# A written list of 1905 numbers takes the place of the planner that ordered a linear-attention and FFN kernel

## The chip, the core and the metric

The kernel runs on one core of one Trainium2 chip. The metric is the device time of one execution in microseconds (us); less is better. A core has five engines that run side by side, each with an instruction queue of its own: PE (TensorE, matrix products), DVE (VectorE), ACT (ScalarE), POOL (GpSimd) and SP (SyncE, which here only issues DMAs). In the source they are called `PE`, `V`, `A`, `G` and `Q`.

## The reference

```python
def _A_ref(x, wqkv, w_phi, wo):
    B, S, D = x.shape; H = 32; Dh = D // H
    q, k, v = (x @ wqkv).reshape(B, S, 3, H, Dh) ...          # 2048 rows of 512, 32 heads of 16
    pq = jnp.einsum("bhsd,hdf->bhsf", q, w_phi)
    pk = jnp.einsum("bhsd,hdf->bhsf", k, w_phi)
    phi_q = jnp.concatenate([_softmax(pq), _softmax(-pq)], axis=-1)
    phi_k = jnp.concatenate([_softmax(pk), _softmax(-pk)], axis=-1)
    kv = jnp.einsum("bhsf,bhsd->bhfd", phi_k, v)
    z  = jnp.einsum("bhsf->bhf", phi_k)
    num = jnp.einsum("bhqf,bhfd->bhqd", phi_q, kv)
    den = jnp.einsum("bhqf,bhf->bhq", phi_q, z)[..., None] + 1e-6
    return (num / den) ... @ wo

def _B_ref(x, w1, b1, w2):                                     # F = 1792
    h = jnp.einsum("bsd,df->bsf", x, w1) + b1
    sp = jnp.log1p(jnp.exp(-jnp.abs(h))) + jnp.where(h > 0, h, 0)
    return jnp.einsum("bsf,fd->bsd", h * jnp.tanh(sp), w2)

x  = A_x                       # (1, 2048, 512)
xn = _layernorm(x)
return x + _A_ref(xn, ...) * silu(_B_ref(xn, ...))
```

All arrays are float32.

## The kernel before

The 2048 rows of `x` are 16 tiles of 128. Each float32 factor of a large product is split into a high and a low part of a shorter format, and each product is three matmuls (low by high, high by low, high by high), mostly 128x512 to a call; 1944 such calls make up nearly all of PE's work. The products for keys and values and both layers of the FFN are done with seven half-sized products in place of eight, so that sums and differences of tiles and of weights (`ts`, `ws`, `wss`, `w1s`, `w2s`) are needed, and each of these is split in its turn: ACT writes the high part (`th`, `w1sh`), and DVE or POOL subtracts it to get the low part (`tl`, `wss`, `w1sl`, `w`).

The stages, in the order in which PE goes through them: first the weights are folded (`wkf`, `wqf`) and the 16 tiles are normalized (`norm`, L517 on) and transposed on PE (`pt`, then `xT`); among and after these come the projections (`k`, `q`, `v`, and `kx`, `ky`, `kz`) and the sums over keys (`kvp`); then FFN layer one (`fx`, `fy`, `fz`), whose transposed inputs go out to DRAM and come back as `fb0h` to `ft3l`; then layer two (`y`, `z`, `x`), mixed with the attention's numerators (`pn`) and output products (`pw`, which read `oh` and `ol`); last `u` and `xx`, the joining of both branches.

In `norm`, DVE finds mean and variance (`st`, `mv`), adds a constant (`rs`), POOL takes the power -1/2 of `rs`, DVE computes `nb` = -mean times `rs` (L528 on, a `scalar_tensor_tensor` of 128x1), and ACT or DVE normalizes the tile; with ACT that is one activation with `nb` as its bias. Only then can PE transpose the tile.

What sets the order: the body doesn't issue anything. Each call on an engine is recorded (`Program.call`, L110); calls inside `one()` (L132) become one operation, and where these calls are on two engines, the operation can run on either: `either` is DVE or POOL, `copy` is ACT or DVE. There are 1905 operations. `ORDER` (L38) names the parts of the work in a row, and so fixes the order in which operations are recorded. PE's operations keep that order. For the four other engines `simulate` (L178) goes through the program with a cost for each operation and picks, whenever an engine is free, the operation whose latest start is earliest; of two engines that can do an operation, the one that gets to it first takes it, and DVE's bid for one that POOL can do counts as 8000 ns later (`PEN`). `issue` (L345) then emits all operations in the order of their simulated starts; their instructions all carry line 352. On the chip each engine goes through its row strictly in order and waits where an input isn't there yet.

Of the kernel before, what the change touches and what calls it, by code (L numbers as in the profile page):

```python
# [54 lines left out]

class Program:


    def __init__(self, nc):
        self.eng = {"PE": nc.tensor, "V": nc.vector, "G": nc.gpsimd, "A": nc.scalar, "Q": nc.sync}  # L60
        self.ops, self.tag, self.cap, self.pe = [], {}, {}, []
        self.group, self.slack, self.part, self.half = None, SLACK, None, 0

    @staticmethod
    def cost(e, m, a, k):
        aps = [v for v in a if isinstance(v, bass.AP)]
        n = aps[0].free_size()
        if e == "PE":
            if m == "transpose":
                return 109  # L70
            n, c = aps[2].free_size(), aps[1].free_size()
            if aps[1].dtype == F32R:
                return max(n / 2.4 + 0.104 * c, c * 0.835 + 2)
            full = 2 * max(n / 1.2 + 2.5, c * 0.835)
            if aps[1].shape[0] == 32:
                return max(full / 16, 27)
            return max(full * aps[0].shape[0] / P, 27)
        if e == "Q":
            return 450
        if e == "A":  # L80
            return (60 if aps[1].space == "PSUM" else 110) + 0.833 * n + 93 * (len(aps) - 2)
        psum = any(v.space == "PSUM" for v in aps[1:])
        nn = max(v.free_size() for v in aps)
        if e == "V":
            if m == "reciprocal":
                return 70 + 6.3 * n
            if m in ("tensor_scalar", "tensor_copy") and not psum:
                return 70 + 0.52 * n
            return 70 + 1.04 * nn
        if k.get("op") == ALU.pow:  # L90
            return 520
        return (140 + 1.73 * n) if bcast(a) else (140 + 2.17 * n)

    @staticmethod
    def records(m, a, k):

        return 2 if m == "transpose" or a[1].dtype == F32R else 4

    def add(self, impl, reads, writes, sets=()):
        o = Op()  # L100
        o.code = sum(self.records(*c) for c in impl["PE"][1]) if "PE" in impl else 0
        o.impl, o.reads, o.writes, o.idx, o.sets, o.slack = impl, reads, writes, len(self.ops), sets, self.slack
        o.pos, o.part, o.half = len(self.pe), self.part, self.half
        self.half = 0
        o.lock = {e for e, (_, calls) in impl.items() if any(locks(e, m, a) for m, a, k in calls)}
        if "PE" in impl:
            self.pe.append(o)
        self.ops.append(o)

    def call(self, e, m, a, k):  # L110
        aps = [v for v in list(a) + list(k.values()) if isinstance(v, bass.AP)]
        w = {box(aps[0])}
        r = {box(v) for v in aps[1:]}
        c = self.cost(e, m, a, k)
        s = [ACT_SET[a[2]]] if e == "A" and a[2] in ACT_SET else []
        if self.group is None:
            self.add({e: (c, [(m, a, k)])}, r, w, s)
        else:
            g = self.group
            g[0].setdefault(e, [0, []])  # L120
            g[0][e][0] += c
            g[0][e][1].append((m, a, k))
            g[1].update(r)
            g[2].update(w)
            g[3].extend(s)

    def halves(self, k):

        self.group[0]["PE"][0] += SWITCH[k]
        self.half = SWITCH[k]  # L130

    @contextmanager  # L132
    def one(self):
# [6 lines left out]
        g, self.group = self.group, None  # L140
        self.add({e: tuple(v) for e, v in g[0].items()}, g[1], g[2], g[3])

    def order(self):
        at = [0]
        for o in self.pe:
            at.append(at[-1] + o.impl["PE"][0])
        self.links()
        return self.simulate(at)

    def links(self):  # L150
        ops = self.ops
        wr, rd = {}, {}
        for o in ops:
            o.succ, dep = [], set()
            for n in o.reads:
                dep.update(i for i, m in wr.get(n[0], ()) if meet(n, m))
            for n in o.writes:
                dep.update(i for i, m in wr.get(n[0], ()) if meet(n, m))
                dep.update(i for i, m in rd.get(n[0], ()) if meet(n, m))
            dep.discard(o.idx)  # L160
            if "PE" in o.impl:
                dep = {d for d in dep if "PE" not in ops[d].impl}
            for d in dep:
                ops[d].succ.append(o)
            o.deps = len(dep)
            for n in o.reads:
                rd.setdefault(n[0], []).append((o.idx, n))
            for n in o.writes:
                wr.setdefault(n[0], []).append((o.idx, n))
        self.uses, self.first = {}, {}  # L170
        for o in ops:
            o.tiles = {n[0] for n in o.reads | o.writes if n[0] in self.tag}
            for n in o.tiles:
                self.uses[n] = self.uses.get(n, 0) + 1
                if n not in self.first:
                    self.first[n] = o
# [917 lines left out]
```

## Time and profile before

| | before |
|---|---|
| median of 3 runs | 507.02 us (506.91 to 510.05) |
| the profiled execution | 507.63 us |
| its span, first to last instruction | 505.6 us |
| PE busy | 488.1 us (97%), 3126 matmuls and transposes |
| DVE busy | 430.8 us (85%), 571 instructions |
| POOL busy | 396.8 us (78%), 264 instructions |
| ACT busy | 280.6 us (56%), 418 instructions |
| DMA | 115.54 MB, mean 229 GB/s |
| mean granted TensorE clock | 0.992 |

The span is what the profile shows of the profiled execution; 2.0 us of its time lie outside it. Busy times are sums of durations. Those of PE are modelled at their ends, and DVE's overlap a little from one instruction to the next, so that a sum can come out above what the engine was really taken for. "Idle before" stands in square brackets in the timeline, with the name of what ended it.

### The profile page before, as it was taken

What the parts mean: (1) busy time and instruction counts of PE and PEld (TensorE: products, weight loads), DVE (VectorE), ACT (ScalarE), POOL (GpSimd) and SP (SyncE); (2) the same over time, 40 slices, a digit from 0 to 9 for tenths busy, and PEclk for the clock granted to TensorE, in tenths of its full rate; (3) what the DMA queues carried; (4) which work ended last, traced back from release to release, by engine and by line L of the source; (5) the groups of instructions that cost most, each with busy time, mean ns of one, the idle gap of its engine ahead of it and who ended that gap; (6) DMA issues with size and microseconds to landing.
All of it is one profiled execution on the core that took longest, in us unless ns stands there. A gap on an engine that the chain in (4) does not pass through costs nothing.

```text
span 505.6 us, 8592 instructions
## 1 busy us (share of the span) xinstructions
PE 488.1 (97%) x3126; PEld 399.4 (79%) x3126; DVE 430.8 (85%) x571; ACT 280.6 (56%) x418; POOL 396.8 (78%) x264
## 2 busy tenths in 40 slices
PE   9986999999999899999999999999999999999993
PEld 9765888888888787888888877888888886788882
DVE  5988899999998869978999898998668568779993
ACT  4864745555354335245423587566796657758420
POOL 2797766989999777657978796977895578799990
PEclk9999899999999999999999999999999999999998
DMA  8775562445683989997899697275964934476375
GB/s 311 244 260 189 198 221 102 160 153 209 219 290 93 324 300 287 288 331 251 278 320 351 202 361 284 83 244 186 312 204 132 376 124 154 148 246 210 105 216 178
DMA packets 64985, 115.54 MB, mean 229 GB/s; under 512 B 6960, under 2 KB 31152, under 8 KB 64944
## 3 DMA queue, kind: packets, MB, share of 16 engines
q1 hardware_dynamic: 64800, 114.98, 66.3%
q8 instruction: 24, 0.39, 0.3%
q14 instruction: 17, 0.14, 0.1%
q10 hardware_dynamic: 144, 0.03, 0.0%
HBM read 72.92 MB, written 42.07 MB: 227 GB/s over the span
## 4 chain that ended last, share of the span: by engine, by line
PE 86%; DVE 7%; ACT 2%; POOL 1%; DMA 1%; issue 0%; ACTq 0%
PE y L352 19%; PE fx L352 14%; PE pw L352 9%; PE fy L352 8%; PE x L352 7%; PE kx L352 7%; PE q L352 7%; PE ky L352 4%; PE fz L352 3%; PE pn L352 2%; PE z L352 2%; PE kz L352 2%; PE kvp L352 2%; DVE nb L352 1%; DMA ft1l<-scrT 1%; PE wake L352 1%
## 5 line engine op out<-in xcount | busy, mean ns | idle before, releaser
L352 PE MATMUL q<-wqh,xT 128*128 128x512 f32 x128 | 43.3, 404 | 0.0
L352 ACT ACTIVATE r<-r,b1t 128x512 f32<-128x512 f32 x56 | 37.9, 714 | 9.1 <-DMA r<-hd 8.8
L352 PEld LDWEIGHTS q<-wqh,xT 128*128 128x128 f32 x128 | 24.8, 194 | 5.2
L352 PE MATMUL q<-wql,xT 128*128 128x512 f32 x64 | 25.6, 400 | 0.0
L352 POOL TENSOR_TENSOR rs<-rs,mhalf 128x1 f32<-128x1 f32 x16 | 10.9, 685 | 12.7 <-DVE rs L352 12.7
L352 ACT ACTIVATE hb<-fx 128x512 f32<-128x512 f32 x14 | 8.3, 597 | 22.4 <-PE fx L352 20.2
L352 DVE TENSOR_REDUCE tz<-ez 128x64 f32<-128x1024 f32 x16 | 19.4, 1211 | 0.4 <-POOL ez L352 0.3
L352 ACT ACTIVATE hc<-fx 128x512 f32<-128x512 f32 x13 | 7.8, 598 | 18.7 <-PE fx L352 18.7
L352 PE MATMUL kx<-wss,th 128*128 128x512 f32 x56 | 17.3, 390 | 0.0
L352 POOL TENSOR_TENSOR w<-w2r,w 128x512 fp32r<-128x512 f32 x11 | 16.1, 1477 | 0.6 <-ACT w L352 0.6
L352 ACT ACTIVATE qs<-q 128x512 f32<-128x512 f32 x15 | 8.8, 589 | 13.8 <-PE q L352 12.4
L352 ACT ACTIVATE hd<-fx 128x512 f32<-128x512 f32 x13 | 7.6, 594 | 15.2 <-PE fx L352 13.0
L352 ACT ACTIVATE x<-x,nb,rs 128x512 f32<-128x512 f32 x13 | 10.6, 814 | 9.4 <-DVE nb L352 9.4
L352 ACT ACTIVATE so<-pw 128x512 f32<-128x512 f32 x14 | 8.3, 593 | 13.5 <-PE pw L352 8.5
L352 ACT ACTIVATE v<-kx 128x512 f32<-128x512 f32 x14 | 8.3, 592 | 13.0 <-PE kx L352 10.4
L352 ACT ACTIVATE ha<-fx 128x512 f32<-128x512 f32 x14 | 8.3, 596 | 12.5 <-PE fx L352 10.2
L352 PE MATMUL pt<-ident,x 128*128 128x128 f32 x64 | 9.6, 277 | 5.6 <-ACT x L352 5.6
L352 ACT ACT_TABLE_LOAD x11 | 14.1, 1283 | 1.4 <-PEq L1086 1.2
L352 PEld LDWEIGHTS q<-wql,xT 128*128 128x128 f32 x64 | 12.4, 194 | 2.7 <-DVE wql L352 0.2
L352 PEld LDWEIGHTS pt<-ident,x 128*128 128x128 f32 x64 | 7.3, 140 | 8.5 <-ACT x L352 7.6
L352 DVE TENSOR_TENSOR hc<-hc,fy 128x512 f32<-128x512 f32 x14 | 9.4, 668 | 5.1 <-ACT hc L352 5.0
L352 POOL TENSOR_TENSOR w1s<-w1a 128x256 f32<-128x256 f32 x11 | 9.7, 888 | 5.0 <-DMA w1a<-w 3.1
(852 smaller groups left out, 1991.1 us busy)
## 6 DMA issues: line engine op xcount, KB each, us to landing
r<-hd SPq DMA_DIRECT2D x28, 512.0 KB, 4.8
x<-x SPq DMA_DIRECT2D x16, 256.0 KB, 4.8
scr<-xT SPq DMA_DIRECT2D x8, 512.0 KB, 2.9
scrT<-th SPq DMA_DIRECT2D x8, 512.0 KB, 2.6
scrT<-tl SPq DMA_DIRECT2D x8, 512.0 KB, 3.5
qd<-qs SPq DMA_DIRECT2D x16, 256.0 KB, 2.1
qp<-qd SPq DMA_DIRECT2D x16, 256.0 KB, 5.8
so<-so SPq DMA_DIRECT2D x16, 256.0 KB, 2.1
```

The source lines that it names most:

```text
L352: getattr(e, m)(*a, **k)
```

## The change

`SCHED`, a text of 1905 numbers, gives the order. A number is the place of an operation in the record; a letter behind it (`V`, `G`, `A`) says which engine does it where there is a choice. `issue` walks through the list and emits. The planner goes with all that fed it: costs, latest starts, links between operations, `halves`, `box`, `locks`. Since the list also holds PE's operations, PE need no longer follow the record; `ORDER` is rearranged too (the same parts).

```diff
-PEN, HOLD, MARGIN = 8000, 300, 1000
...
+SCHED = """
+26 13 0 19 1 45 2 15 3 73 4 16 5 17 27 6 18 7 28 95 14 8 9 10 29 121 20 30 31 127 46 23 32A 118 47 48 33 49 37 74 147
...
+1862 1888V 1865 1889 1892 1895 1901 1896V 1897V 1902V 1898 1903G 1904
+"""
...
     def issue(self):
-        first = True
-        for o in self.order():
-            for m, a, k in o.impl[o.eng][1]:
+        left, first = set(range(len(self.ops))), True
+        for s in SCHED.split():
+            i = int(s.rstrip("VGA"))
+            left.remove(i)
+            op = self.ops[i]
+            e = s.lstrip("0123456789") or next(iter(op))
+            for m, a, k in op[e]:
...
     def norm(t):
...
-        V.scalar_tensor_tensor(nb, mv[:, 0:1], -1.0, rs, op0=ALU.mult, op1=ALU.mult)
+        V.tensor_scalar(nb, mv[:, 0:1], -1.0, rs, op0=ALU.mult, op1=ALU.mult)
...
     def den(t):
...
-        V.tensor_tensor(tz, tz, r, op=ALU.mult)
+        either(tz, tz, r, op=ALU.mult)
...
-        V.tensor_tensor(r3, r3, dn[:, :, None].to_broadcast([P, H, 2]), op=ALU.mult)
+        either(r3, r3, dn[:, :, None].to_broadcast([P, H, 2]), op=ALU.mult)
```

PE's work is the same in number and kind. Choices fall otherwise: counted over both programs, DVE gets 25 more copies of 128x512 and one of 128x256, 35 more two-input operations of 128x512 from SBUF, 9 of 128x1024, 3 of 128x768, 11 of 128x256, and 6 of 128x256 with an input from PSUM; 15 of 64 columns and 2 normalizations of 128x512 leave it. POOL loses 35, 9, 3 and 17 of 512, 1024, 768 and 256 columns and gains the 15 of 64. ACT loses 23 activations of 512 columns and one of 256, and its loads of function tables go from 11 to 15.

Three places in the rows of the engines follow. In names, the number behind the last `_` counts tiles and differs between the two programs.

The first is DVE's row around the tiles whose transposes come sixth and seventh, some 45 us into the program. `nb` is the bias of the normalization, `rs` and `mv` its inputs, `k0s`, `k1s`, `k0r`, `k1r` belong to a softmax of keys, `ts` to sums of tiles. Before:

```order
L352 TENSOR_SCALAR rs_237<-mv_236 128x1
L352 TENSOR_TENSOR ts_220<-xr_219,pt_186 128x256
L352 TENSOR_TENSOR xT_227<-pt_229,xT_227 128x512
L352 BN_STATS st_246<-x_245 128x6
L352 BN_AGGR mv_247<-st_246 128x2
L352 SCALAR_TENSOR_TENSOR nb_239<-mv_236,rs_237 128x1
L352 TENSOR_SCALAR rs_248<-mv_247 128x1
L352 TENSOR_TENSOR ts_220<-pt_186,ts_220 128x256
L352 TENSOR_REDUCE k0s<-k0e 128x64
L352 RECIPROCAL k0r<-k0s 128x64
L352 TENSOR_REDUCE k1s<-k1e 128x64
L352 SCALAR_TENSOR_TENSOR nb_250<-mv_247,rs_248 128x1
```

And now:

```order
L158 TENSOR_SCALAR nb_241<-mv_238,rs_239 128x1
L158 BN_STATS st_294<-x_293 128x6
L158 BN_AGGR mv_274<-st_273 128x2
L158 BN_STATS st_323<-x_322 128x6
L158 BN_AGGR mv_295<-st_294 128x2
L158 BN_AGGR mv_324<-st_323 128x2
L158 TENSOR_SCALAR nb_251<-mv_248,rs_249 128x1
L158 TENSOR_SCALAR nb_262<-mv_259,rs_260 128x1
L158 TENSOR_SCALAR rs_296<-mv_295 128x1
L158 TENSOR_TENSOR xT_216<-pt_218,xT_216 128x512
```

The `nb` are of another form, and the statistics of later tiles (`st_294`, `st_323`) stand between them: DVE is further ahead with the normalization relative to PE than it was.

The second is SP's row where it loads the inputs of FFN layer one. `ft1h` and `ft1l` are high and low part of one of them, `fb..` and the other `ft..` further ones, `qd` and `scr` writes to DRAM. Before:

```order
L352 DMA w1a_493<-w 128x1024
L352 DMA fb2h_483<-scr_101 128x4x256
L352 DMA fb2l_484<-scr_101 128x4x256
L352 DMA ft0h_485<-scrT_104 128x4x256
L352 DMA ft0l_486<-scrT_104 128x4x256
L352 DMA ft1h_487<-scrT_104 128x4x256
L352 DMA ft1l_488<-scrT_104 128x4x256
```

And now:

```order
L158 DMA fb0h_478<-scr_100 128x4x256
L158 DMA fb1h_480<-scr_100 128x4x256
L158 DMA qp_601<-qd_110 128x512
L158 DMA ft1l_487<-scrT_104 128x4x256
L158 DMA qp_512<-qd_107 128x512
L158 DMA fb1l_481<-scr_100 128x4x256
L158 DMA ft0h_484<-scrT_104 128x4x256
L158 DMA qd_109<-qs_453 128x512
L158 DMA qd_116<-qs_451 128x512
L158 DMA scr_103<-xT_379 128x2x256
L158 DMA ft2l_489<-scrT_104 128x4x256
L158 DMA ft0l_485<-scrT_104 128x4x256
```

`ft1l` has moved from the end of that row to a place near its start, ahead of `fb2h`, `fb2l` and `ft0h`.

The third is PE's row behind the third of the four `pn` operations, up to the first product that reads the new `oh` and `ol`. Before:

```order
L352 MATMUL pn_3_998<-ph_734,kvw 32x256
L352 MATMUL y_0_993<-mb8h,w2sa_971 128x512
L352 MATMUL y_0_993<-mb8l,w2sa_971 128x512
L352 MATMUL y_0_993<-mb8h,w2sa_971 128x512
...
L352 MATMUL x_1_903<-mb8h,w2sa_971 128x512
L352 MATMUL pw_1008<-oh_0_999,wo0l 128x512
L352 MATMUL pw_1008<-ol_0_1000,wo0h 128x512
```

And now:

```order
L158 MATMUL pn_3_1004<-ph_721,kvw 32x256
L158 MATMUL y_0_999<-mb7h,w2sa_861 128x512
L158 MATMUL y_0_999<-mb7l,w2sa_861 128x512
...
L158 MATMUL y_1_1000<-mb9h,w2sa_942 128x512
L158 MATMUL pw_1017<-oh_0_1007,wo0l 128x512
L158 MATMUL pw_1017<-ol_0_1008,wo0h 128x512
```

Between `pn` and `pw` stood 12 matmuls; now there are 24.

More of the change, by code (lines that the diff above doesn't have):

```diff
@@ L52 @@
-class Op:
-    __slots__ = ("impl", "reads", "writes", "at", "idx", "succ", "ndep", "late", "ready", "start", "eng", "sets", "slack", "open", "soon", "pos", "deps", "lock", "part", "half", "code", "tiles")
+wq1 N0 wk0 N4 wk1 N1 K0 wq0 Ka1 Q4 wv0 wv1 V0 N5 N2 ws0 Q0 Q2 N8 Q5 ws1 N12 N3 V4 Q8 Kb1 Q1 N6 Q12 ws2 Ka3 N7 Ka2 Kc1
+N9 ws3 Kb2 N10 Q6 Kd1 Kc2 Q9 N13 N11 N14 Kd2 Kb3 N15 Ka5 Ka4 Kc3 Ka7 K4 Kd3 Ka6 Kb4 Kb6 Kc4 Q11 Kc6 Q14 Kd4 Kb5 Q13 A0
+P2 A1 Q10 Q3 Kd6 A2 A3 P1 A4 Kc5 Q7 Kb7 Q15 Kd5 L0 P0 Kc7 Fa2 Kd7 Fa1 S1 P3 Fa3 Fa0 S0 Fb1 Fc1 Fb2 Fb0 Fd1 Fc2 Fb3 Fc3
@@ new lines @@
+90G 124 106 155 44A 123V 108G 91 218 233 139 162 189 184G 597 190 171 141V 55 159 210 156 83 125 172 140V 142 163V
+116A 109G 228 92 191 110 173 165 93 211 174 272 175A 94G 234 166 143 324 273 325 192 212 274 193A 136 229 275 126A
+256V 185 144G 194 167A 176 111 195 180 168 230A 235 196 177 181 213A 178 198A 423 186G 112 64 199 214 137 221 182V 307
+236 222 237 308 160V 238A 215 317G 225 200V 223V 201V 252 145 326 226V 117 202 239 309 113G 276 216 277A 253 358 318
+243V 278 240 310 291 282A 327 203 244 246G 241 219 328 257 245V 242 378 224 283 146 259 258G 284V 205 179 286 247 261
@@ new lines @@
+559 419A 435 289 457 436G 446 386 467 412V 405G 387 437V 447 470 438 448 439 472 431 440G 471A 376 432 164 456A 505
+413V 482 468V 506A 473 414 483 449V 458 450G 517 459 347G 451 415 507 518V 406 422 290 461G 416 398 484V 474 523 469
+476G 452 493 417G 453 503 460 407 486 462G 485 519 560G 636 494 463 475 487G 520 496 477G 495 526 521A 508 497G 524A
+464 478 441 530 454G 183 465 255 479 547 488G 525 527 498V 466G 489 509 549 548A 504V 480 531A 556 537 499 598G 490
+511G 564 533 491 550A 492V 589 561V 557G 538 558 500 570 565V 528A 562G 522 645 442 540 691 609 481G 532 510 534 539
@@ new lines @@
+610A 512G 541V 649 579 535A 568V 571 563V 590V 710 552 529 569V 612 591V 542V 633 592G 580 582 572 634A 581 513 501
+551 573V 543 502G 696 553 544 566 635 637 693G 514 575 583G 545 593 600G 546V 596 850 644 611 608 683 515 638 576 516V
+641 601V 616 577A 584V 602 578 594V 574 613 585 433 599V 595V 617A 618 554A 614A 603V 650G 646 536 623 606V 651G 619
+684 624 658 567G 642 643 626 555 586 678 615 639 604 652G 659V 620 692G 653V 694G 661 660 685 607G 587 666 662V 711
+676 697V 695V 663 677A 625 621A 605V 686G 679A 622 700 648 656 712 640 667 680 654 588V 725 655V 627G 647 687V 718
@@ new lines @@
+992 988V 1085 942G 962 1082 1003 1083 1118 1000A 946 867 994V 985G 943 1001 993 959 944 947A 965G 949 1005 1084 963
+950 806 986G 1007 966 995G 989 1034 1012 976G 996 967V 977V 1006A 1014 978 990V 934 844 1013A 1008 915 968 945 979G
+969 970V 1025 1009A 997 980 1028 971V 1030 1089 1029A 1017G 972 1026A 1096 1027 1042 998 1104 891 981G 1093 964 1018
+1049 1015 1016 1019G 1055 1036G 1050A 1091 1044V 1053 1095 1035 1094 1020 1021 1060 1043 1054A 1126 1022G 1037G 960A
+1097 1105A 1098 1056 1045G 1031 1023V 1143 1057A 1061A 1119 1046 1062 1110 1051 1088 1099G 1047 1052 1160 1004 1066G
@@ new lines @@
+1111A 924 1038 1120 1024 1137 1010 1074G 1181 1063 1092 1048 1144A 1087 1058 1244 1115 1039 1100G 1106 1067 1117 1101
+1068V 1075 1107 1116A 1127 1064 1076G 1140 1161A 1129V 1138A 1165 1069 1077 1353 1070 1065 1071V 1130 1072G 1086 1167
+1166A 1078 1330 1040 1011 1141 1112 1131G 1079G 961 1132 1102 1080G 1172 1108 1246 1168 1081 1190 1121G 1145 1122V
+1152G 1103 1123 1113 1162 1146 1133 1148 1163 1173A 1182 1216 1169V 1186 1134V 1170 1135G 1153 1178 1109 1441 1184
+1253G 1136 1175 1114 1245 1179 1174 1124 1176A 1128G 1335 1147 1187A 1125 1193 1059 1149A 1188 1150 1185V 1151 1289
@@ new lines @@
+1408 1427 1400V 1429 1425 1306V 1472 1481 1307 1377 1473 1315 1401 1409 1493 1474 1669 1530 1325V 1424 1444 1436 1402V
+1507 1430V 1449 1326 1422 1450 1322 1423 1380V 1432 1457 1475V 1445G 1393 1434 1323 1520 1381 1299 1433 1437 1342
+1382V 1476 1458G 1516 1482 1431 1459G 1438G 1446 1531 1477 1451 1532V 1517V 1447 1483 1383 1518V 1489 1384 1478 1535
+1394V 1495 1439V 1488 1601 1452V 1479 1529 1440 1509 1630 1508 1454 1484G 1494 1521 1453 1496 1460 1486 1565 1497V
+1679 1490V 1485 1385V 1522 1386V 1498 1510 1463V 1499 1536 1511G 1461 1501 1566 1491V 1523 1558 1500 1395G 1631 1537
@@ new lines @@
+1762V 1734 1711V 1767V 1735 1779V 1799 1740V 1782 1683 1764 1741V 1781V 1768 1783G 1744 1718A 1769V 1720 1763 1736
+1811 1804 1770 1730V 1793 1719 1759V 1742 1686 1801V 1784 1805V 1785 1788A 1721V 1722V 1790 1789A 1786V 1831 1745V
+1743V 1746G 1851 1812V 1807 1747 1737A 1794V 1723 1738 1814 1827 1787V 1748V 1815 1808 1771V 1724V 1842 1750V 1823
+1802V 1791A 1772V 1806 1819 1795V 1792 1816V 1803 1796 1813 1820V 1839 1818 1751V 1828V 1752 1890 1817 1797V 1773
+1753V 1809A 1845 1846 1822 1852V 1810 1824V 1866 1821 1840V 1774V 1867 1825 1832V 1854 1863 1848G 1829 1860 1843V 1873
@@ L56 @@
+1833 1878 1849V 1872 1850 1826 1837 1879 1835 1857 1891V 1868 1874 1899 1869V 1884 1870V 1875V 1871 1830 1855V 1893
+1876G 1858V 1861V 1834 1859 1864G 1841 1836 1877 1880 1885 1844 1881G 1894 1853 1882V 1838 1856 1883 1886 1900 1887G
+1862 1888V 1865 1889 1892 1895 1901 1896V 1897V 1902V 1898 1903G 1904
+"""
 class Program:
@@ L60, in __init__ @@
         self.eng = {"PE": nc.tensor, "V": nc.vector, "G": nc.gpsimd, "A": nc.scalar, "Q": nc.sync}
[L61 to L108, printed above, removed]
@@ L110, in call @@
-    def call(self, e, m, a, k):
[L111 to L115, printed above, removed]
+        self.ops, self.group = [], None
+    def call(self, e, m, a, k):
         if self.group is None:
-            self.add({e: (c, [(m, a, k)])}, r, w, s)
+            self.ops.append({e: [(m, a, k)]})
         else:
[L119 to L125, printed above, removed]
@@ L127, in halves @@
-    def halves(self, k):
-        self.group[0]["PE"][0] += SWITCH[k]
-        self.half = SWITCH[k]
+            self.group.setdefault(e, []).append((m, a, k))
     @contextmanager
@@ L137, in one @@
             return
-        self.group = ({}, set(), set(), [])
+        self.group = {}
         yield
[L140 to L176, printed above, removed]
@@ L345, in issue @@
-    def issue(self):
-        first = True
-        for o in self.order():
-            for m, a, k in o.impl[o.eng][1]:
-                e = self.eng["A" if first and m == "dma_start" else o.eng]
-                first = first and m != "dma_start"
-                getattr(e, m)(*a, **k)
-def box(v):
-    step, parts = v.ap[0]
-    if v.space == "DRAM":
-        return v.tensor.name, 0, 1, 0, 1
-    lo, row = v.offset % step, v.offset // step
-    return v.tensor.name, lo, lo + sum((n - 1) * st for st, n in v.ap[1:]) + 1, row, row + parts
@@ L364, in meet @@
-def meet(a, b):
-    return a[1] < b[2] and b[1] < a[2] and a[3] < b[4] and b[3] < a[4]
-def locks(e, m, a):
-    if e == "G":
-        return True
-    aps = [v for v in a if isinstance(v, bass.AP)]
-    if e != "V" or any(v.space == "PSUM" for v in aps):
-        return False
-    return aps[0].free_size() > 1 if m in ("tensor_scalar", "tensor_copy") else len(aps) > 2
-def bcast(a):
-    return any(st == 0 and n > 1 for v in a if isinstance(v, bass.AP) for st, n in v.ap)
+        self.ops.append(self.group)
@@ new lines, in one @@
+        self.group = None
+    def issue(self):
+        left, first = set(range(len(self.ops))), True
[5 more added lines that the diff above has]
+            for m, a, k in op[e]:
+                g = self.eng["A" if first and m == "dma_start" else e]
+                first = first and m != "dma_start"
+                getattr(g, m)(*a, **k)
+        assert not left
@@ L408, in bank @@
         t = psum.tile(shape, F32, tag="ps", name=name)
-        prog.tag[t.tensor.name] = "ps"
         return t
@@ L413, in alloc @@
         t = pools[tag].tile(shape, dtype, tag=tag, name=name)
-        prog.tag[t.tensor.name] = tag
         return t
@@ L1055, in block_kernel @@
     for c in ORDER.split():
-        prog.part = c
         if c in parts:
```

225 lines of the change are left out of this document (44 added, 181 removed).

## The prediction

> **What bounds the kernel now.** I read the page's shares and the chain of waits first, to see which engine sets the time, then PE's waits, then the clock by stage.
>
> ```profile
> PE 488.1 (97%) x3126; PEld 399.4 (79%) x3126; DVE 430.8 (85%) x571; ACT 280.6 (56%) x418; POOL 396.8 (78%) x264
> PE 86%; DVE 7%; ACT 2%; POOL 1%; DMA 1%; issue 0%; ACTq 0%
> 368.09 16.32 PE y L352 x72
> PE pt L352 <- ACT x L352: 5.6, 6, 2.1
> PE fx L352 <- DMA ft1l<-scrT: 1.3, 1, 1.3
> PE wake L352 <- DVE mhalf L465: 1.1, 1, 1.1
> PE v L352 <- DVE wv1l L352: 0.5, 1, 0.5
> PE pw L352 <- DVE ol L352: 0.5, 1, 0.5
> PE pw L352 <- ACT oh L352: 0.4, 1, 0.4
> 0.00:50.56 50.56, 43.26 (x236) 36.55 (x237) 41.24 (x81) 30.81 (x48) 33.85 (x35) 1.00 0.69 251
> 50.56:63.20 12.64, 12.64 (x54) 10.24 (x53) 10.51 (x15) 9.40 (x15) 8.91 (x7) 0.87 0.51 198
> 63.20:303.36 240.16, 238.88 (x1650) 196.07 (x1648) 220.91 (x318) 114.08 (x168) 197.39 (x133) 1.00 0.74 250
> 303.36:417.12 113.76, 113.76 (x619) 93.54 (x618) 87.59 (x92) 79.97 (x110) 85.38 (x48) 1.00 0.62 216
> ```
>
> PE is the bound: 86% of the chain is PE, and in the quiet stretch of the third row 72 matmuls follow each other in 16.32 us, 0.227 us each. 1944 of them are 440.7 us. With the transposes, folded weights and small products at their own spacings I get 481.0 us of work for PE. Its first matmul starts at 1.12 us and its last would end at 482 without a gap; it ends at 497.7. So 15.5 us of the span is lag, and no order of work can take more than that from PE.
>
> Where it arises: PE's waits, without the 1.1 us before the first matmul, sum to 8.3 us, two thirds in transposes (`pt`) that wait for the normalized tile, all in the first 50 us. Just behind them the granted clock stands at 0.87 for 12.64 us, which costs 12.64 x 0.13 = 1.6 us. That makes 9.9 us with a name. The other 5.6 is spread in pieces below a microsecond (starts after a gap, changes between the small products and the large); I find no edit that is aimed at it.
>
> The two largest waits have one history:
>
> ```profile
> 44.00 4.67 POOL L352 TENSOR_TENSOR wss<-ws,wss 128x1024 fp32r<-128x1024 f32 x2
> 44.52 1.87 DVE L352 SCALAR_TENSOR_TENSOR nb<-mv,rs 128x1 f32<-128x1 f32 x1
> 46.31 0.17 DVE L352 BATCH_NORM_AGGREGATE mv<-st 128x2 f32<-128x6 f32 x1
> 46.41 2.29 DVE L352 SCALAR_TENSOR_TENSOR nb<-mv,rs 128x1 f32<-128x1 f32 x1
> 48.73 0.81 ACT L352 ACTIVATE x<-x,nb,rs 128x512 f32<-128x512 f32 x1 [1.49 <-DVE nb L352]
> 47.29 0.66 PE L352 MATMUL pt<-ident,x 128*128 128x128 f32 x4 [2.08 <-ACT x L352]
> 49.59 0.66 PE L352 MATMUL pt<-ident,x 128*128 128x128 f32 x4 [1.64 <-ACT x L352]
> ```
>
> An operation on one column takes DVE 1.87 and 2.29 us, exactly as long as POOL's two `wss` (2.34 each) go on. ACT starts when `nb` is there, PE when ACT is done. These two are 3.7 of the 5.6 us.
>
> **The change part by part.**
>
> *The new form of `nb`.*
>
> ```profile
> L352 DVE SCALAR_TENSOR_TENSOR nb<-mv,rs 128x1 f32<-128x1 f32 x16 | 10.7, 678 | 0.0
> L352 DVE TENSOR_SCALAR rs<-mv 128x1 f32<-128x1 f32 x16 | 2.3, 145 | 0.2
> L352 DVE TENSOR_SCALAR x<-x,mv,rs 128x512 f32<-128x512 f32 x3 | 1.5, 536 | 0.0
> ```
>
> The nearest row to the new `nb` is `rs`: same engine, operation and shape, 16 times at a mean of 145 ns, so no wait beside POOL in a single one of them. DVE saves 10.7 - 2.3 = 8.4 us; on the path this takes the delay out of the six waits for `x`, and the list also draws DVE's statistics ahead of the transposes. The bounds are 0 (the wait passes to the next two-input operation on DVE, or to POOL's power of `rs`) and the whole 5.6 us; I take 4.8, since a first tile or two still have only their own chain to wait for. With no gaps of 1.6 and 2.1 us in a row I take the 0.87 clock to go too: 1.6 us. If one gap of 2 us stays, that comes back with it.
>
> [...]
>
> *The loads.*
>
> ```profile
> 161.29 0.52 SPq L352 DMA_DIRECT2D ft1h<-scrT  x1
> 162.68 0.52 SPq L352 DMA_DIRECT2D ft1l<-scrT  x1
> 168.48 0.50 PE L352 MATMUL fx<-ft1l,w1sh 128*128 128x512 f32 x1 [1.28 <-DMA ft1l<-scrT]
> ```
>
> `ft1l` lands 5.8 us after its issue and is late by 1.28. It now stands in front of `fb2h`, `fb2l` and `ft0h`. Counted along PE's work, it is issued about 22 us ahead of its use, `ft1h` about 11. Each is above the 5.8 us, so the wait goes: 1.3 us. What is moved back (`fb2h`, `fb2l`) is read by later products; that `qp` loads now stand among them costs a slot of 0.5 us each on SP. Bounds: -1.3 and, if another of the eight comes late by one issue of 1.4 us, 0.
>
> *`pn` and `pw`.*
>
> ```profile
> 432.70 0.49 PE L352 MATMUL pw<-oh,wo0l 128*128 128x512 f32 x1 [0.37 <-ACT oh L352]
> 433.67 0.50 PE L352 MATMUL pw<-ol,wo0h 128*128 128x512 f32 x1 [0.47 <-DVE ol L352]
> ```
>
> With 24 matmuls (5.4 us) in place of 12 (2.7 us) between them, both waits of 0.84 us together are covered: 0.9. Bounds 0 and 0.9.
>
> *More work for DVE.* This is the price.
>
> ```profile
> L352 DVE TENSOR_TENSOR hc<-hc,fy 128x512 f32<-128x512 f32 x14 | 9.4, 668 | 5.1 <-ACT hc L352 5.0
> L352 DVE TENSOR_TENSOR w<-w2r,w 128x512 fp32r<-128x512 f32 x3 | 3.3, 1092 | 1.6 <-ACT w L352 1.6
> L352 DVE COPY so<-pw 128x512 f32<-128x512 f32 x2 | 1.4, 692 | 0.3 <-PE pw L352 0.3
> L352 DVE TENSOR_REDUCE tz<-ez 128x64 f32<-128x1024 f32 x16 | 19.4, 1211 | 0.4 <-POOL ez L352 0.3
> L352 DVE TENSOR_TENSOR tl<-ts,th 128x1024 fp32r<-128x1024 f32 x5 | 10.8, 2160 | 0.0
> L352 DVE SCALAR_TENSOR_TENSOR den<-tz 128x32 f32<-128x32 f32 x16 | 7.7, 485 | 0.2
> L352 POOL TENSOR_TENSOR w<-w2r,w 128x512 fp32r<-128x512 f32 x11 | 16.1, 1477 | 0.6 <-ACT w L352 0.6
> L352 ACT ACT_TABLE_LOAD x11 | 14.1, 1283 | 1.4 <-PEq L1086 1.2
> ```
>
> DVE with an input from PSUM takes 0.668 us for 512 columns (`hc`); with both from SBUF it takes 1.092 (`w`), and 1024 columns take 2.160 (`tl`) where a reduce over as many takes 1.211. The differences, 0.42 and 0.95, are what the neighbourhood of POOL adds. So the 25 copies are 25 x 0.692 = 17.3; 35 operations of 512 are 23.4 to 38.2; 9 of 1024, 10.9 to 19.4; 3 of 768, in proportion, 2.7 to 4.9; 17 of 256, at half of 512, 5.7 to 9.3. That is 60 to 89. `nb` takes off 8.4, two normalizations 1.1, the 15 of 64 columns 3 to 7 (`rs` and `den` as bounds, with some rounding up): 44 to 77 more, 475 to 508 in all. The sum overlaps itself: `mv` starts at 46.31, takes 0.17, and the next starts at 46.41, so 0.07 each; with some 640 instructions DVE is really taken for 430 to 463 us, less than PE's 481. On the whole program it fits. In the stretch from 63 to 303 us it is narrow: there 220.91 less 318 x 0.07 is 199 of 240.16 us now, and I count 22 us of undisturbed work more, 92% of the stretch. Where DVE's results are needed by PE, the list leaves it 13 us of room at 111 us, 18 at 177, 25 at 243 and 32 at 302, with undisturbed durations; before it was 35 to 50 from 170 on. Some 85 two-input operations lie there now (81 before, whose mean excess over undisturbed ones of their size I count as 0.35 us). With POOL relieved I take 0.3: 25 of the 32 us. I take 1.5 us of lost time for single places that come short; bounds 0 and the 10 to 15 us of the rival below.
>
> *ACT* gets four more table loads of 1.28 us against 24 activations fewer. It is busy for 56%, and they lie at 260 to 360 us: nothing.
>
> *The end.*
>
> ```profile
> 497.06 1.34 ACT L352 ACTIVATE u<-x 128x512 f32<-128x512 f32 x2 [4.08 <-PE x L352]
> 498.43 0.69 DVE L352 TENSOR_TENSOR u<-u,sr 128x512 f32<-128x512 f32 x1 [3.83 <-ACT u L352]
> 500.48 0.69 DVE L352 TENSOR_TENSOR xx<-u,xx 128x512 f32<-128x512 f32 x1
> ```
>
> After the last matmul DVE does four operations one by one (498.43 to 501.17). Now the last addition goes to POOL. Its nearest row is POOL's `w`, 1.48 us for 512 columns beside a busy DVE, and less here, where DVE is idle: I estimate 1.1; one step of 0.69 less in the row for DVE, one slower step, and two chains that now end beside each other: -0.3, bounds +0.8 and -0.7.
>
> Sum: -4.8 - 1.6 - 1.3 - 0.9 + 1.5 - 0.3 = -7.4. Against the profiled execution, 507.63, that is 500.2; the median of the runs lies 0.6 below that execution, so 499.6.
>
> **The rivals.** *All lag goes.* PE's operations are interleaved more finely, so that small pieces vanish too: 507.63 - 15.5 - 0.6 = 491.5. Against it: the pieces at `pn` and `kvp` are changes of PE's own work, which stay.
>
> *DVE takes the bound between 110 and 300 us, slower.* [...] Where the mean excess of a two-input operation in that stretch passes 32 / 85 = 0.38 us, PE waits for low parts and sums (`w1sl`, `w`, `hc`). `w` has 0.42 and `tl` 0.95. At 0.55 us it is 47 against 32, 15 us late; with 8.9 us gained elsewhere: 499.6 - 1.5 + 15 = 513. [...] At 0.45 us it is 6 late, 504: no change.
>
> *The order doesn't do it.* The waits at the start go over to weights or to `xT` (for instance `v` for `wv1l`, 0.5 us now): gains of 2 to 4 us, 503 to 505.
>
> **How the numbers follow.** The forecast (497 to 502) has 0.50, all lag gone 0.14, DVE late by some microseconds 0.12 and no gain at the start 0.10 (both 502 to 508), DVE late by more 0.14 (511 to 516). Within 1% of the median is 501.95 to 512.09, about what a measurement of this kernel can tell from no change. Faster: 0.14 and nearly all of 0.50, 0.62. Slower: most of the last, 0.12. The same: 0.26. The range takes all but the slower case and a little: 491.5 to 508.5.
>
> **What would show it.** Right: `nb` at 0.15 us each, no `pt` wait above 1 us, a granted clock of 1.00 from 50 to 63 us, no wait for `ft1l`; DVE busy between 470 and 510 us with POOL at about 310. Wrong: rows in PE's waits that name DVE (`w1sl`, `hc`, `w`, `ol`) between 110 and 310 us with sums above 3 us, or a `pt` or weight wait of 2 us at the start, with the low clock behind it.

## The result, and the profile after

The changed kernel takes 500.40 us (median of 4 runs, 499.53 to 500.77) against 507.29 us for the kernel before beside it: a ratio of 0.985, with a 95% interval of 0.9813 to 0.9887. It is faster by 6.9 us. The profiled execution took 500.49 us with a span of 498.8.

The page's first row of the changed kernel:

```profile
PE 485.6 (97%) x3126; PEld 396.8 (80%) x3126; DVE 429.4 (86%) x644; ACT 268.0 (54%) x398; POOL 296.3 (59%) x215
```

The six longest of PE's nine waits in it (us in total, times, longest):

```profile
PE wake L158 <- DVE mhalf L241: 1.1, 1, 1.1
PE pt L158 <- ACT x L158: 0.8, 1, 0.8
PE kx L158 <- DVE kp L158: 0.8, 1, 0.8
PE fy L158 <- DVE ha L158: 0.8, 1, 0.8
PE ky L158 <- DVE v L158: 0.5, 1, 0.5
PE fz L158 <- ACT zb L158: 0.5, 1, 0.5
```

Besides the 1.1 us before the first matmul, only 0.8 us for `x` are left of the old waits; `ft1l`, `wv1l`, `oh` and `ol` are gone. In their place stand seven short waits that are new, 0.3 to 0.8 us each, five of them for DVE. The windows, by the same stretches as before (us; then PE, weight loads, DVE, ACT and POOL busy; granted clock; DMA share; GB/s):

```profile
0.00:50.56 50.56, 49.35 (x273) 42.68 (x274) 43.02 (x100) 33.76 (x52) 36.56 (x36) 1.00 0.64 230
50.56:63.20 12.64, 12.64 (x60) 9.92 (x58) 12.20 (x26) 8.00 (x13) 9.14 (x4) 1.00 0.74 290
63.20:303.36 240.16, 235.82 (x1742) 191.17 (x1741) 224.73 (x328) 105.54 (x161) 164.53 (x120) 1.00 0.75 251
```

In the first 50.56 us PE does 273 matmuls and transposes where it did 236, and the clock behind them is 1.00 where it was 0.87. From 63 us on it is the other way: PE was busy for 238.88 of 240.16 us before and is for 235.82 now.

The lag (start of a matmul, less 1.1 us, less the PE work ahead of it, as in the prediction) tells the same by place. It is an estimate, since it rests on the spacings that were taken for PE's work. The table holds it for the two kernels and for some of the experiments below, at times of the execution:

| lag in us at | 50 us | 100 us | 175 us | 200 us | 425 us | last matmul | from there to the span's end |
|---|---|---|---|---|---|---|---|
| before | 7.8 | 9.7 | 11.9 | 13.1 | 12.8 | 15.5 | 8.3 |
| after | 0.1 | 4.7 | 6.3 | 8.7 | 8.9 | 9.2 | 7.7 |
| e1 (before, new `nb`) | 2.6 | 3.1 | 5.5 | 6.6 | 7.6 | 9.0 | 8.3 |
| e2 (after, old `nb`) | 4.2 | 9.6 | 12.2 | 13.9 | 15.6 | 16.1 | 7.3 |
| e9 (e1 with two moves) | 3.0 | 3.5 | 3.9 | 5.1 | 6.0 | 6.6 | 9.6 |
| e11 (after, mended) | 0.8 | 2.1 | 2.5 | 5.9 | 6.7 | 6.7 | 7.3 |

The changed kernel gains 7.7 us up to 50 us, loses 2.7 of it again between 50 and 100, and is ahead by some 6 at the end.

Three groups of DVE's instructions, after (count, then busy us and mean ns, then idle before):

```profile
L158 DVE TENSOR_SCALAR nb<-mv,rs 128x1 f32<-128x1 f32 x16 | 3.1, 196 | 0.9 <-POOL rs L158 0.9
L158 DVE TENSOR_TENSOR w<-w2r,w 128x512 fp32r<-128x512 f32 x10 | 6.8, 702 | 1.2 <-ACT w L158 1.2
L158 DVE TENSOR_TENSOR w1sl<-w1s,w1sh 128x1024 fp32r<-128x1024 f32 x3 | 4.5, 1503 | 0.0
```

The last of them before:

```profile
L352 DVE TENSOR_TENSOR w1sl<-w1s,w1sh 128x1024 fp32r<-128x1024 f32 x3 | 6.3, 2103 | 0.5 <-ACT w1sh L352 0.4
```

`nb` takes 196 ns in the mean. And DVE, with 73 instructions more, is busy for a little less than before (429.4 against 430.8 us): `nb` saves 7.6 us, and the two-input ones got shorter, `w` from 1092 to 702 ns and `w1sl` from 2103 to 1503.

### The profile page after: what moved, and what is told of

It reads as the page before. It is cut to its first block, busy times and chain, and to the rows that moved or that the text cites. A ratio compares the mean times of both kernels' runs of the same rounds, so it can differ in the third digit from the quotient of the medians.

```text
span 498.8 us, 8534 instructions
## 1 busy us (share of the span) xinstructions
PE 485.6 (97%) x3126; PEld 396.8 (80%) x3126; DVE 429.4 (86%) x644; ACT 268.0 (54%) x398; POOL 296.3 (59%) x215
## 4 chain that ended last, share of the span: by engine, by line
PE 75%; DVE 8%; ACT 5%; issue 4%; POOL 3%; DMA 3%; SPq 0%; POOLq 0%; DVEq 0%; ACTq 0%
PE y L158 16%; PE fx L158 12%; PE pw L158 8%; PE q L158 8%; PE fy L158 6%; PE kx L158 5%; PE x L158 5%; PE ky L158 3%; PE fz L158 3%; PE pn L158 2%; PE pt L158 1%; DMA sr<-so 1%; PE v L158 1%; PE z L158 1%; PE kvp L158 1%
## 5 line engine op out<-in xcount | busy, mean ns | idle before, releaser
L158 POOL TENSOR_TENSOR tl<-ts,th 128x1024 fp32r<-128x1024 f32 x7 | 17.6, 2521 | 3.7 <-ACT th L158 3.7
L158 ACT ACTIVATE x<-x,nb,rs 128x512 f32<-128x512 f32 x15 | 12.2, 814 | 10.0 <-DVE nb L158 8.7
L158 POOL TENSOR_TENSOR h<-h,sr 128x512 f32<-128x512 f32 x3 | 7.4, 2478 | 17.1 <-DMA sr<-so 16.9
L158 DVE TENSOR_TENSOR ol<-pn,oh 128x256 fp32r<-128x256 f32 x32 | 11.8, 413 | 4.3 <-ACT oh L158 4.2
L158 ACT ACTIVATE hb<-fx 128x512 f32<-128x512 f32 x11 | 6.5, 592 | 14.7 <-PE fx L158 11.1
L158 POOL TENSOR_TENSOR rs<-rs,mhalf 128x1 f32<-128x1 f32 x16 | 8.6, 549 | 9.4 <-DVE rs L158 9.4
L158 ACT ACTIVATE w<-w2r 128x512 fp32r<-128x512 f32 x14 | 8.7, 630 | 9.9 <-DMA w2r<-w 3.8
L158 ACT ACTIVATE oh<-pn 128x256 fp32r<-128x256 f32 x32 | 10.6, 394 | 6.0 <-issue 2.5
L158 DVE BATCH_NORM_STATS2 st<-x 128x6 f32<-128x512 f32 x16 | 10.9, 685 | 3.1 <-DMA x<-x 3.1
L158 DVE TENSOR_TENSOR xT<-pt,xT 128x512 fp32r<-128x512 f32 x16 | 10.9, 684 | 2.8 <-ACT xT L158 2.8
L158 ACT ACTIVATE w1sh<-w1s 128x1024 fp32r<-128x1024 f32 x7 | 7.4, 1059 | 11.0 <-POOL zacc L158 8.5
```

Source lines behind the costliest of these rows:

```text
L158: getattr(g, m)(*a, **k)
```

## The experiments

All kernels below are built as lists in the manner of the change; `SCHED` can say any order and any engine. The order that the planner found was written out as such a list too; it gives the same rows as the kernel before. "Operations" are those of the list; 235 of the 1905 are on another engine in the two kernels (120 from POOL to DVE and 71 from DVE to POOL, 34 from ACT to DVE and 10 back), so 49 more than before are on DVE instead of POOL. The 64 in two expectations below count otherwise: they are the 35, 9, 3 and 17 that POOL loses, without the 15 of 64 columns that it gains.

### e1 and e2: the form of `nb`, without the list and the list without it

```diff
 # e1: SCHED is the order and the engines of before
-V.scalar_tensor_tensor(nb, mv[:, 0:1], -1.0, rs, op0=ALU.mult, op1=ALU.mult)
+V.tensor_scalar(nb, mv[:, 0:1], -1.0, rs, op0=ALU.mult, op1=ALU.mult)
```

> The order and the engine choices of before, written out as a list, so that every row is the old one; the only change is the new form of nb (tensor_scalar in place of scalar_tensor_tensor). [...] Rival (the list's order did it, by drawing the statistics ahead): another wait takes nb's place at once, time above 505.5 us.

Measured: 501.14 us (500.00 to 501.55) against 507.67, ratio 0.9873 (0.9844 to 0.9901). PE's waits in e1, without the 1.1 us before the first matmul and 0.3 for `wv1l`:

```profile
PE fx L158 <- DMA ft1l<-scrT: 1.6, 1, 1.6
PE pt L158 <- ACT x L158: 1.4, 2, 0.8
PE pw L158 <- DVE ol L158: 0.5, 1, 0.5
PE pw L158 <- ACT oh L158: 0.4, 1, 0.4
```

Its `nb`, and its second window:

```profile
L158 DVE TENSOR_SCALAR nb<-mv,rs 128x1 f32<-128x1 f32 x16 | 3.0, 201 | 0.3 <-POOL rs L158 0.2
```

```profile
50.56:63.20 12.64, 12.64 (x59) 10.47 (x58) 12.64 (x14) 7.50 (x12) 10.07 (x6) 1.00 0.64 248
```

One line alone brings 6.5 of the 6.9 us. The waits for `x` fall from 5.6 to 1.4, the low clock goes, and the waits for `ft1l`, `ol` and `oh` stand much as they were: the order is the old one. The rival is out.

```diff
 # e2: SCHED is that of the changed kernel
-V.tensor_scalar(nb, mv[:, 0:1], -1.0, rs, op0=ALU.mult, op1=ALU.mult)
+V.scalar_tensor_tensor(nb, mv[:, 0:1], -1.0, rs, op0=ALU.mult, op1=ALU.mult)
```

> The changed kernel with nb in its old form, all else as in the changed kernel. [...] Rival (order): the list keeps DVE far enough ahead that a slow nb costs less than 1.5 us, time below 502.

Measured: 506.60 us (505.99 to 509.09), ratio to before 0.9986 (0.9967 to 1.0004). The rival, below 502 us, is out. Without the new form the list can't be told from the old kernel. DVE's timeline in e2, then POOL's (start, duration), and the wait of PE that follows:

```profile
43.73 2.35 DVE L158 SCALAR_TENSOR_TENSOR nb<-mv,rs 128x1 f32<-128x1 f32 x1
...
46.09 2.95 DVE L158 TENSOR_TENSOR wss<-ws,wss 128x1024 fp32r<-128x1024 f32 x1
```

```profile
43.67 2.39 POOL L158 TENSOR_TENSOR ws<-wkr,ws 128x1024 f32<-128x1024 f32 x1
46.02 1.93 POOL L158 TENSOR_TENSOR k1e<-k1e,k1r 128x1024 f32<-128x1024 f32 x1
```

```profile
PE pt L158 <- DVE qs L158: 2.3, 1, 2.3
```

`nb` started 0.06 us after POOL's `ws` and took 2.35 us, as long as `ws` itself; `wss` was then caught in the same way by `k1e`. The wait went on to PE with 2.3 us, and the 12.64 us behind it had a clock of 0.86. Four of the 16 `nb` take 1.5 us or more in e2. So the form of an operation on one column decides what a list of 1905 places is worth.

### e3 and e4: the order and the choice of engines apart

```diff
 # e3: the order of the changed kernel, each operation with the engine it had before
 # e4: the order of before, each operation with the engine it has in the changed kernel; both with the new nb
```

> The order of the changed kernel, but each operation on the engine that before gave it: 64 operations go back from DVE to POOL, and the copies go back to ACT. [...]

> The order of before, with nb in its new form, but each operation on the engine that the list gives it: DVE gets the copies and the 64 operations of POOL. [...] Theory B (order): DVE gets more work in a row that was not laid out for it and PE waits for it between 63 and 303 us; 4 us or more above e1.

Measured: e3 541.84 us (ratio 1.0676, 1.0629 to 1.0723), e4 528.95 us (1.0423, 1.0394 to 1.0452). The page's first row of each:

```profile
PE 499.1 (93%) x3126; PEld 398.9 (74%) x3126; DVE 408.6 (76%) x571; ACT 281.4 (52%) x422; POOL 380.5 (71%) x264
```

```profile
PE 495.9 (94%) x3126; PEld 399.1 (76%) x3126; DVE 453.9 (86%) x644; ACT 267.0 (51%) x394; POOL 300.8 (57%) x215
```

In neither is DVE, ACT or POOL busy above 86%, and both are more than 27 us slower than e1. My reading, which no run isolates, is that each engine's row is laid out for the work that it holds; put an operation on another engine at the same place and it waits, in order, for what isn't there yet. For DVE's operations with two inputs from SBUF I count an excess over an undisturbed one of their size of 0.48 us each before, 0.40 in e3, 0.30 in e4 and 0.18 after. The choice of engines makes more of the drop than the order, and it takes both; but e3 and e4 are stretched by their waits, which alone spreads the two engines apart, so the shares are not to be read closely. The time of e4 is 27.8 us above that of e1: there theory B holds, far beyond the size that it names (4 us or more above e1).

### e5 to e7: pieces of the two lists joined

```diff
 # e5: the changed kernel's list up to 55 us of PE's work, then what is left in the order of before
 # e6: the order of before up to 50 us, then what is left in the changed kernel's
 # e7: the changed kernel's up to 55 us, that of before up to 145 us, then the changed kernel's
```

> The list's order and choices for the operations up to 55 us of PE's work, then all that is left in the order and on the engines of before; nb in its new form. Theory (the list's head takes 2.6 us of lag off the start, its middle from 60 to 100 us gives 4.6 us back through DVE): about 2.5 us below e1, 498 to 499.5 us, lag near 0 at 50 us and no wait for DVE above 0.5 us between 60 and 100 us. Rival (the debt of DVE is made in the head itself, which puts off work): the same waits for k5e, kp and v show up behind the seam and the time stays at 500.5 or more.

> The other way round: the order and choices of before for the operations up to 50 us of PE's work, then the list's; nb in its new form. Theory: the head's 2.6 us of lag and the list's 9 us behind 50 us add up, 502.5 to 504 us. Rival (debt made in the head): the waits at 70 to 100 us go and the time is 500 us or less.

> The list up to 55 us of PE's work, the order and choices of before up to 145 us, then the list again. If the pieces add up by their lag in the two traces (0.1 + 0.7 + 4.0 us): 495 to 497 us, below both kernels. If the seams cost what the list's middle costs: 499.5 us or more.

Measured: e5 505.24 us (ratio 0.9953, 0.9933 to 0.9974), e6 514.08 (1.0114), e7 512.99 (1.0103). The theory was missed in all three; the rivals of e5 (500.5 us or more) and e7 (499.5 us or more) name open bounds, and these hold. The longest waits of PE, e5, e6, e7 in turn:

```profile
PE q L158 <- DVE xT L158: 2.7, 1, 2.7
```

```profile
PE kx L158 <- DVE ts L158: 4.6, 1, 4.6
PE kx L158 <- DVE kp L158: 3.6, 1, 3.6
```

```profile
PE fz L158 <- DVE kp L158: 5.1, 1, 5.1
PE pz L158 <- POOL zacc L158: 2.8, 1, 2.8
PE q L158 <- DVE xT L158: 2.7, 1, 2.7
```

Single waits behind the seams cost 2.7 to 5.1 us each, more than the stretches were worth that were to be exchanged. The rival of e5, that the list's head puts work off, is borne out as to the size but hardly as to the names: PE waits 2.7 us for `xT`, 0.8 for `v`, 0.2 for `kp` and not at all for `k5e`. In e6 the debt should have gone, and it didn't; so "a debt made in the head" isn't the whole of it either. What the three show is that in none of these joins could the lag of a stretch be cut out of one list and added to another.

### e8: the changed kernel again

> The changed kernel again, beside the others, to set it against e1 (the new nb alone, 501.1). Theory (the list as such is worth little): 500 to 501 us.

Measured: 500.27 us (498.96 to 500.41), ratio 0.9843 (0.9815 to 0.9870). Against e1, 501.14 us with a ratio of 0.9873, the intervals overlap: beyond the one line the list is worth somewhat under 1 us, and these runs can't tell it from nothing.

### e9: the two small terms alone

```diff
 # SCHED of e1; SP's row, the second half of one load group
-fb2h fb2l ft0h ft0l ft1h ft1l
+ft0h ft1h ft1l ft0l fb2h fb2l
 # PE's row behind the third pn: groups of six matmuls, up to the first pw
-Gb8 Gb8 pw(O8)
+Gb8 Gb8 Gb9 Gb9 pw(O8)
```

> e1 (order and engines of before, new nb) with two small moves: the loads of ft0h, ft1h, ft1l and ft0l stand ahead of fb2h and fb2l in SP's row, and two more matmul groups of layer two stand between the third pn and its first pw, as in the list. Theory (these are the prediction's two smaller terms, and hold for themselves): the wait for ft1l (1.6 us in e1) and the two for oh and ol (0.9) go, about 2.5 to 3 us below e1: 498 to 499 us, below both kernels. Rival (what is moved back comes late in its place): the waits turn up under another name, 500.5 us or more.

Measured: 500.02 us (499.96 to 501.65), ratio 0.9857 (0.9825 to 0.9890). All three waits are gone from PE's list, and only 0.3 us for `w2sa` are new:

```profile
PE pt L158 <- ACT x L158: 1.3, 2, 0.7
PE wake L158 <- DVE mhalf L241: 1.1, 1, 1.1
PE v L158 <- DVE wv1l L158: 0.5, 1, 0.5
PE y L158 <- DVE w2sa L158: 0.3, 1, 0.3
```

PE ends 2.4 us earlier than in e1 (lag 6.6 against 9.0), as was expected, yet the time falls by 1.1 only, and the runs of the two overlap. 1.3 us are lost at the end. The chain of waits there:

```profile
484.12 5.15 DMA so<-so
489.26 0.02 issue
489.28 2.91 DMA sr<-so
492.19 0.02 issue
492.22 0.70 DVE u L158
```

The last product of the attention goes to DRAM and comes back as `sr`; that takes 8 us, and now it ends 1.3 us after DVE wants it. In e1 the same way was hidden behind PE.

### e12: an earlier way for the last `sr`

```diff
 # SCHED of e9
-Gd7 Gd8 Gd9 pw(O10) Gd10 ...
+pw(O10) Gd7 Gd8 Gd9 Gd10 ...
```

> e9 with the last of the output products (pw of O10), its copy and its write to DRAM moved ahead of four other groups. Theory (in e9 PE ends 2.4 us earlier than in e1, but the last sr comes back from DRAM at 492.2 us, 1.3 us after it is wanted): the last u waits for PE alone, 498.3 to 499.2 us. Rival (the last transfers out set the end): 499.6 or more.

Measured: 498.76 us (497.95 to 499.97), ratio 0.9812 (0.9758 to 0.9866). The time is in the expected band, but not for that reason: `so` is still issued at 483.95 us and DVE still waits for `sr`. ACT's row in e12:

```profile
482.23 0.60 ACT L158 ACTIVATE so<-pw 128x512 f32<-128x512 f32 x1 [3.79 <-DMA out<-xx]
```

PE has done the product by 479.5 us, but the copy starts only when an `out` transfer ends, after 3.79 us in which ACT is idle; and SP, whose row is in order too, issues `so` 1.1 us after the copy, behind a load that waits for POOL. The cause is not mended, the span (498.2 us, in an execution of 499.97) is not below that of e9 (498.0), and the intervals of the two overlap. No gain is shown.

### e10 and e11: the changed kernel's own waits mended

```diff
 # SCHED of the changed kernel (number and engine)
-355A 321V 356 342V ... 341 ... 382
+355A 382 321V 356 341 342V ...
 # copies of v, kp, kp, hb and hc, from DVE back to ACT
-468V 518V 484V 729V 745V
+468A 518A 484A 729A 745A
 # 431 and 432 (xT of tile 15) to before 435 and 437; 703 (ha) to before 673
 # e10 only: 762V and 763G (the last zacc) to before 778 and 779G; 802, 800 (pz), 803, 801 (zb) to before 769 and 793
```

> The changed kernel with the places mended at which its trace shows PE waiting: nb of the eleventh tile and a reduce ahead of k5e; the high and low part of the fifteenth tile ahead of work that isn't urgent; five copies (v, kp, kp, hb, hc) from DVE back to ACT, which is idle there; ha ahead of three others; the last two sums zacc, and pz after them, earlier. Theory (the lag of 9 us in its trace is made of DVE's and ACT's rows holding back single results between 70 and 200 us): 3 to 5.5 us less, 495 to 497.5 us. Rival (each mend only passes the wait on, as the seams did): 499.5 us or more.

Measured: 500.09 us (497.62 to 500.53), ratio 0.9838 (0.9805 to 0.9871): no better than the changed kernel. But its lag at 175 us is 2.0 us where it was 6.3; what was won there goes at one place. PE's row at that place, and two windows of e10:

```profile
190.96 2.08 PE L158 MATMUL pz<-zacc,ones 128*128 128x512 f32 x2 [2.83 <-ACT zb L158]
```

```profile
175.00:205.00 30.00, 27.17 (x282) 21.05 (x281) 25.76 (x33) 8.27 (x14) 18.76 (x15) 0.89 0.72 225
189.00:202.00 13.00, 11.04 (x34) 8.21 (x35) 10.94 (x12) 4.34 (x7) 7.18 (x5) 0.74 0.70 214
```

`pz`, moved ahead, waits 2.8 us, and the clock behind it is at 0.74 for 13 us: 13 x 0.26 = 3.4 us more. It need not come: one of e10's four executions had a mean clock of 0.997, against 0.989 in the profiled one, and took 497.62 us. e11 leaves out that last mend.

> e10 without its last mend (the sums zacc and pz stand where the changed kernel has them), the other mends kept. Theory (e10's first mends took PE's lag at 175 us from 6.3 to 2.0 us, and only the moved pz gave it back, by a wait of 2.8 us and a low clock behind it): the lag stays near 2 us up to 185 us, rises by 1.7 at pz and ends near 5; 495 to 497 us. Rival (the end of the kernel hangs on the way of sr through DRAM and not on PE): PE ends 4 us earlier, but the time falls by less than 1.5 us, 499 or more.

Measured: 496.75 us (496.34 to 497.57), ratio 0.9780 (0.9734 to 0.9825). That is the fastest kernel here, faster than before by 10.5 us and than the changed kernel by 3.6. The ranges of their runs lie apart (up to 497.57 here, from 498.96 in the changed kernel and e8), though the intervals of the ratios still touch. Its longest waits:

```profile
PE wake L158 <- DVE mhalf L241: 1.1, 1, 1.1
PE pz L158 <- POOL zacc L158: 1.0, 1, 1.0
PE fz L158 <- ACT zb L158: 0.6, 1, 0.6
PE z L158 <- POOL ma10l L158: 0.3, 1, 0.3
```

The waits for `kp`, `v`, `ha` and `x` are gone. The span's part after the last matmul (7.3 us) didn't grow, so here the end still hangs on PE.

## Why the prediction was right, and where its steps were not

**What bounds the kernel, and how much there is to gain.** Right. PE was busy 97% before and after, and the lag of 15.5 us held as the ceiling: the best kernel has 6.7 left of it.

**The new form of `nb`** (-4.8 and -1.6). Right in mechanism and size: e1 gives 6.5 us for it alone, with the `nb` at 0.2 us (0.15 was said) and the clock at 1.00; e2 loses 6.2 by undoing it. The longest of the 16 took 215 ns after, where in e2, in the old form, four take 1.5 us or more. e2's longest, begun 0.06 us after `ws`, ended 0.02 us after it: there the later one waited.

**The loads** (-1.3) and **`pn` and `pw`** (-0.9). Right. The waits are gone after, and e9 takes them off by themselves, for 2.4 us of lag in all. What the prediction did not ask is whether the end still hangs on PE once such a piece is saved; in e9 it doesn't, and the end grows by 1.3 us.

**More work for DVE** (+1.5, forecast busy sum 475 to 508 us). This is the step that was mis-sized, on both sides. Busy came out at 429.4. What the sum left out is that the operations that DVE had already would get shorter too. It added prices to the old 430.8 us, in which 170 operations with two inputs from SBUF hold an excess of 0.48 us each, 82 in all. After, 213 of them hold 0.18 each, 38 in all. Before, the 13 two-input operations of 512 columns that no operation of POOL overlaps took 0.69 us at most, the 140 others up to 2.90; what in POOL's neighbourhood makes the difference, no run shows. With another order and less work on POOL the collisions became fewer, and the sum kept them. In the stretch from 63 to 303 us, where 0.3 was taken in place of 0.35, I count some 0.2.

The busy times were also misread, ahead of the prediction and in it. They are not sums of durations: the traces' durations of DVE add up to 463.8 us before and 470.0 after, and the page's 430.8 and 429.4 have the overlap taken out already. So nothing was to be taken off for it. By durations, the undisturbed work grew by 470.0 - 463.8 + 7.6 (`nb`) + 44 (excess) = 58 us, an estimate; the low side of the sum has 52 to 56 without `nb`, so that part was about right. From 63 to 303 us DVE was busy for 220.91 of 240.16 us before, 92% and not 83%, and is for 224.73 now.

And yet DVE costs more than 1.5 us. By lag it held PE up at 72 to 101 us by 3.3 us and at 173 to 185 us by 1.5; the first lies ahead of the stretch that was named (110 to 300 us). DVE has little room at the first place, but it has as little in e1, where PE has no wait there. The windows of the changed kernel and of e1:

```profile
64.00:102.00 38.00, 35.30 (x159) 27.79 (x158) 36.32 (x57) 17.93 (x27) 27.13 (x21) 1.00 0.70 264
64.00:102.00 38.00, 38.00 (x234) 31.36 (x233) 36.69 (x66) 21.65 (x32) 31.85 (x26) 1.00 0.45 160
```

So busy time, on which that term and its rival rested, doesn't decide it. What the trace shows is the place of single results in an in-order row, as with this `nb`, which stands behind a `k5e` that began just after a long operation of POOL:

```profile
68.21 2.41 POOL L158 TENSOR_TENSOR tl<-ts,th 128x1024 fp32r<-128x1024 f32 x1
68.27 2.90 DVE L158 TENSOR_TENSOR k5e<-kp,k5m 128x512 f32<-128x512 f32 x1
...
71.69 0.20 DVE L158 TENSOR_SCALAR nb<-mv,rs 128x1 f32<-128x1 f32 x1
```

e11 moves five copies and a handful of small operations and takes 3.6 us off the time. It changes places and takes load off DVE (420.4 us) at once, so it doesn't part the two.

**The order of the start.** Not a term of its own in the sum, though the list gains 2.5 us there beyond `nb` (lag at 50 us 2.6 in e1, 0.1 after). That unforeseen gain pays for half of the loss at DVE. By lag, 6.5 us for `nb` (e1), 2.4 for the loads and `pw` (e9) and 2.5 here, less 4.8 at DVE, are 6.6; the lag at the last matmul fell by 6.3. The total, 499.6 against 500.4, is closer than the terms deserve: two misses, 3.3 us at DVE and 2.5 at the start, nearly cancel, and that is luck.

**The end** (-0.3): 7.7 us after the last matmul where it was 8.3, so -0.6.

**ACT at nothing.** Right: it is busy 54%, and no wait of PE names a table load.

**The rivals.** DVE as the bound with a slower kernel did not come. e4 has many waits of the kind that the rival names (3.8 us for `hc` and 5.0 for `kp`, from DVE) and takes 529 us, but with DVE busy for 86%, no more than in the changed kernel. What a move of work between POOL and DVE costs or saves by itself is not shown: putting the operations back in e3 costs 41 us, but e4 shows that the places in the rows alone can cost such sums. "The order doesn't do it" was meant to say that the start doesn't get faster; in another sense it is near to the truth, since without the new `nb` (e2) the list gives 0.14%, and the interval of that ratio takes in no change at all.

## What to carry to other kernels

Look for the smallest instructions that sit on a path and take as long as a large one elsewhere: a 128x1 operation of 2 us named its own remedy, and one line of another form gave what a list of 1905 places was credited with. Order and choice of engine in in-order rows belong together: in five tries (e3 to e7) a part of one schedule in another cost more than the part was worth. Mending the single waits that a trace names worked in e11 and took the waits away in e9, but each mend has to be measured: in e10 and e12 one of them brought nothing. Before a busy sum is priced, take the durations undisturbed, those of the old work too, and treat the collisions as a separate term, since a change that moves work moves the collisions.
